# Identity products in TensorE's first idle stretches, and a later place for five denominator groups, in an attention and feed-forward kernel

## The chip, the cores and the metric

The kernel runs on one NeuronCore of a Trainium2 chip. Its engines work side by side: TensorE (PE; its weight loads are listed as PEld), VectorE (DVE), ScalarE (ACT), GpSimd (POOL), and SyncE (SP), whose queue issues nearly all DMAs here. The metric is the device time of one execution in microseconds (us); the figure given is the median of the runs.

## The reference

Attention with normalised queries and keys over 8 batches, 12 heads, 448 positions and a head size of 64, followed by a feed-forward layer with a squared ReLU; everything is fp32.

```python
def rmsnorm(x, g):
    return x / np.sqrt(np.mean(x * x, axis=-1, keepdims=True) + 1e-06) * g
q_n, k_n = rmsnorm(q, g_q), rmsnorm(k, g_k)          # q, k, v: (8, 12, 448, 64)
scores = (1 / np.sqrt(64)) * q_n @ k_n.transpose(0, 1, 3, 2)
attn = np.exp(scores - scores.max(-1, keepdims=True))
attn = attn / (attn.sum(-1, keepdims=True) + 1e-09)
x = (attn @ v).transpose(0, 2, 1, 3).reshape(8 * 448, 768)
h = np.maximum(x @ w_in, 0.0)                        # w_in: (768, 2048)
return h * h @ w_out                                 # w_out: (2048, 768)
```

## The kernel before

**Pairs and units.** Two neighbouring heads of one batch make a pair, so there are 48 pairs, `i` = 0 to 47, six to a batch. The feed-forward layer works on two batches at a time; such a unit has 12 pairs. Its products use Strassen's scheme: seven products P1 to P7 stand for eight, in `first_products` (L705, x by w_in, seven times three matmuls for each of eight tiles of a unit) and `second_products` (L757 and L786, the hidden values by w_out). An fp32 matmul is two instructions in the trace.

**Order of the work.** All instructions are issued in an order written out by hand (`manual_schedule`), each engine in its own order. First the attention of pairs 0 to 11 runs alone (`visit_alone`, two visits a pair). Then `ffn` is a generator that yields after every product, and `run(until)` takes products from it until a cost is spent; between two calls of `run` stands the attention of a pair of the next unit, in two visits for pairs up to 24 (`visit_among`) and in one for later ones (`visit_whole`). So the attention of pairs 12 to 24 lies among the feed-forward products of the first unit, in which `first` is true. During this unit the kernel also converts the weights: the words of w_in and w_out are loaded by SP (L868, L873), split by ScalarE (L887 to L889), joined by VectorE (L900, L920, L924), combined by VectorE and GpSimd (L946) and stored (L948).

**The start.** Before the program proper, the first rows of q and k are loaded (L157, L166), the identity is made in `ident` by GpSimd, and the gains' product goes into PSUM (L95), from where ScalarE takes it as `g` (L100). `normalize_first` squares a row block (ScalarE, L179), adds it up (VectorE, L192, L195), takes the power -1/2 (GpSimd, L202) and scales q (VectorE, L217). Then each engine reads a flag (L101) and branches (L102) into `program`, which is there twice: with `shift` False, which runs here, and with `shift` True. The program sets up memory and starts more loads, and then comes the stretch that the change touches: `turn(0, 1)` and `turn(0, 0)` transpose k and q of pair 0 on TensorE (L362, L365) into bank 6 and bank 7; kT is copied by ScalarE (L372), and qT is scaled by g on VectorE (L370). `score` (L397) multiplies them, and `weigh` (L405) is ScalarE's exponential. For later pairs, square and normalise run on ScalarE, VectorE and GpSimd (L179, L181, L192, L202, L217), before the pair is turned.

**The denominators.** A pair's weights are added up by GpSimd (`additions`, L424) into two sums. `denominators(i)` (L507) multiplies each sum by a matrix of ones on TensorE, into bank 3 for these pairs, and `take_sums` (L549) transposes that bank on VectorE into `inverse`, in a single buffer that it shares with the squares of a later pair. Two tasks queued by the visit, `invert` (L566, L567) and `finish` (L582), run later and end with the pair's values being multiplied. `attend` (L477) multiplies the weights by v. For `visit_among(i, n)` the order on TensorE is: the denominators of pair i - 1 if n is 1 and they are still missing, two slots of `attend(i - 1)`, then the scores of pair i. A pair with odd i has only slot 2 to score in its second visit, into banks 0 and 1; one with even i has slots 2 and 3, into banks 0 to 3. The products of the feed-forward layer use banks 5, 6 and 7.

The main loop calls `denominators(i - 1)` early, between the two `run` calls that precede the second visit, and then the visit finds `inverse` filled:

```python
run(COST * (2 * x - (2 if whole(i - 1) else 1)) / (2 * unit))
...
if n and first and x > 1 and not shift:
    denominators(i - 1)
run(COST * x / unit)
```

## Time and profile before

| what | value |
|---|---|
| median of 4 runs | 1432.3 us (1431.05 to 1433.89) |
| the profiled execution | 1433.92 us; span of its trace 1432.5 us |
| PE busy | 1408.0 us, 98% of the span |
| DVE, ACT, POOL busy | 659.8, 592.7, 677.0 us |
| chain that ended last | PE 92%, DVE 3% |
| PE busy from 0 to 24 us | 14.78 us |
| PE busy from 140 to 520 us (the first unit's products with attention among them) | 376.39 us |
| L507, denominators | 48 instructions, 151.8 to 475.7 us |

The span runs from the first to the last instruction of the trace; the execution's own time is 1.4 us longer. A row of a timeline has the start, the duration, the engine, the line of the kernel, what it writes and reads, and, in brackets, how long the engine stood idle before it and which work ended that. Instructions of one kind that follow each other are merged into a row, whose duration runs from the start of the first to the end of the last, so that it can overlap the next row a little; the distance from start to start is then the cost of a group.

### The profile page before, as it was taken

Reading aid. Unit: us, or ns where it says so; the run is one execution under the profiler, and the core shown is the slowest. Engines: PE = TensorE matmul, PEld = TensorE weight load, DVE = VectorE, ACT = ScalarE, POOL = GpSimd, SP = SyncE. Lnnn points to the kernel's source line nnn. Section 1 sums busy time; section 2 is a strip of 40 time slices with the busy share of each in tenths; the row PEclk is TensorE's granted clock in tenths of the full one; section 3 lists DMA queues with packets and bytes.
Section 4 is the critical chain, followed back from the end, with each engine's and each line's share of the span. In section 5 each row is a group of like instructions: output and inputs, shape, how many; then the busy total and the mean of one; then the engine's idle time right before and its main releaser. Section 6 shows DMA issues by size and latency. Waiting matters only on the chain.

```text
span 1432.5 us, 15428 instructions
## 1 busy us (share of the span) xinstructions
PE 1408.0 (98%) x4932; PEld 681.6 (48%) x4932; DVE 659.8 (46%) x1233; ACT 592.7 (41%) x1114; POOL 677.0 (47%) x676
## 2 busy tenths in 40 slices
PE   7999999999999999999999999999999999999998
PEld 3333444444444445445454544445454455555554
DVE  5997365877778513324252452324233241132413
ACT  6874566547555244442415234351432303212130
POOL 5666654746556656446445565464462422021111
PEclk9999999999999999999999999999999999999999
DMA  5765346665676663443435464343622232313122
GB/s 144 191 195 150 66 103 185 174 199 142 196 204 200 189 178 95 149 115 118 125 65 175 113 186 125 97 131 77 181 70 89 94 154 78 115 51 127 38 88 80
DMA packets 309279, 188.12 MB, mean 131 GB/s; under 512 B 265796, under 2 KB 293316, under 8 KB 300996
## 3 DMA queue, kind: packets, MB, share of 16 engines
q1 hardware_dynamic: 308896, 186.97, 44.6%
q8 instruction: 41, 0.67, 0.2%
q14 instruction: 50, 0.41, 0.1%
q10 hardware_dynamic: 292, 0.07, 0.0%
HBM read 144.57 MB, written 42.40 MB: 131 GB/s over the span
## 4 chain that ended last, share of the span: by engine, by line
PE 92%; DVE 3%; SPq 1%; issue 1%; ACT 1%; POOL 1%; DMA 1%; DVEq 0%; POOLq 0%; ACTq 0%
PE bank L705 36%; PE bank L786 29%; PE bank L477 10%; PE bank L397 9%; PE bank L757 5%; PE bank L490 1%; PE bank L507 1%; PE bank L516 1%; DVE acc L827 1%; SPq L157 1%; PE bank L362 1%; DMA words<-in_moe_w_out_dram 0%; ACT wT L405 0%; SPq L166 0%; DVE out_sb L946 0%
## 5 line engine op out<-in xcount | busy, mean ns | idle before, releaser
L705 PE MATMUL bank<-xT,in_sb 128*128 128x448 f32 x1344 | 515.4, 542 | 0.0
L705 PEld LDWEIGHTS bank<-xT,in_sb 128*128 128x128 f32 x1344 | 252.4, 190 | 260.4 <-issue 250.9
L827 DVE TENSOR_TENSOR acc<-acc,bank 128x384 f32<-128x384 f32 x324 | 173.7, 549 | 233.0 <-PE bank L786 184.9
L786 PE MATMUL bank<-out_sb,hid 128*128 128x384 f32 x768 | 266.6, 487 | 0.5 <-DVE acc L827 0.5
L725 DVE TENSOR_TENSOR hid<-bank,part 128x448 f32<-128x448 f32 x128 | 76.9, 621 | 330.0 <-PE bank L705 329.7
L405 ACT ACTIVATE wT<-bank,rr 128x448 f32<-128x448 f32 x288 | 161.2, 633 | 124.2 <-PE bank L397 73.2
L786 PE MATMUL bank<-out_sb,sums 128*128 128x384 f32 x576 | 203.9, 490 | 2.7 <-DVE acc L827 2.6
L786 PEld LDWEIGHTS bank<-out_sb,hid 128*128 128x128 f32 x768 | 145.4, 190 | 104.4 <-DVE acc L827 2.4
L202 POOL TENSOR_TENSOR rr<-ms,minus_half 128x8 f32<-128x8 f32 (+1 forms) x96 | 146.3, 1524 | 91.5 <-DVE ms L195 78.8
L741 POOL TENSOR_TENSOR sums<-hid 128x384 f32<-128x384 f32 x32 | 32.3, 1008 | 302.1 <-ACT hid L727 302.1
L397 PE MATMUL bank<-qT,kT 64*128 64x448 f32 (+1 forms) x768 | 164.7, 575 | 1.5 <-DVE qT L370 1.1
L726 ACT ACTIVATE hid<-hid 128x448 f32<-128x448 f32 x128 | 73.3, 573 | 196.8 <-DVE hid L725 196.8
L786 PEld LDWEIGHTS bank<-out_sb,sums 128*128 128x128 f32 x576 | 107.7, 190 | 87.1 <-issue 8.1
L712 ACT COPY part<-bank 128x448 f32<-128x448 f32 x128 | 67.8, 530 | 175.6 <-PE bank L705 175.6
L424 POOL TENSOR_TENSOR sum<-sum,wT 128x448 f32<-128x448 f32 (+1 forms) x96 | 110.4, 1171 | 10.8 <-ACT wT L405 8.1
L397 PEld LDWEIGHTS bank<-qT,kT 64*128 64x128 f32 (+1 forms) x768 | 55.6, 174 | 104.8 <-issue 68.0
L477 PE MATMUL bank<-wT,vt 128*64 128x448 f32 x480 | 102.2, 546 | 0.0
L757 PE MATMUL bank<-out_sb,hid 128*128 128x384 f32 x256 | 85.6, 488 | 0.0
L528 POOL COPY few<-few 32x14 f32<-32x14 f32 x48 | 9.1, 189 | 153.3 <-DVE few L526 151.3
L424 POOL TENSOR_TENSOR sum<-wT 128x448 f32<-128x448 f32 x48 | 57.1, 1208 | 50.4 <-ACT wT L405 50.4
L192 DVE TENSOR_REDUCE ms<-squares 128x8 f32<-128x512 f32 (+1 forms) x68 | 41.8, 615 | 76.4 <-ACT squares L179 76.4
L727 ACT ACTIVATE hid<-hid 128x448 f32<-128x448 f32 x128 | 73.8, 577 | 4.0
(96 smaller groups left out, 1281.5 us busy)
## 6 DMA issues: line engine op xcount, KB each, us to landing
out_sb<-out_forms SPq DMA_DIRECT2D x24, 1536.0 KB, 9.7
in_sb<-in_forms SPq DMA_DIRECT2D x24, 1344.0 KB, 5.8
words<-in_moe_w_in_dram SPq DMA_DIRECT2D x32, 384.0 KB, 3.8
words<-in_moe_w_out_dram SPq DMA_DIRECT2D x32, 384.0 KB, 3.7
out_forms<-out_sb SPq DMA_DIRECT2D x8, 1536.0 KB, 7.0
in_forms<-in_sb SPq DMA_DIRECT2D x8, 1344.0 KB, 6.0
qk<-in_q_dram SPq DMA_DIRECT2D x96, 96.0 KB, 3.3
qk<-in_k_dram SPq DMA_DIRECT2D x96, 96.0 KB, 2.5
```

The lines of the kernel that those rows point to most:

```text
L202: self.nc.gpsimd.tensor_tensor(out=self.rr[i][:, x, 0 : self.count(i)], in0=ms, in1=self.minus_half.to_broadcast(list(ms.shape)), op=ALU.pow,)
L397: nc.tensor.matmul(sc[some], lhsT=turned[p, 1][r, keys], rhs=turned[p, 0][r, :], start=True, stop=True,)
L405: nc.scalar.activation(new_weights((i, m), e), sc, AF.Exp, scale=rows.rr[i][:, 1, 2 * m + e : 2 * m + e + 1],)
L424: nc.gpsimd.tensor_tensor(out=sums[i, e][some], in0=left[some], in1=weights[key_of(i, m), e][some], op=ALU.add)
L477: nc.tensor.matmul(values_bank(i)[ds(e * D, D), :], lhsT=lasts[i % 2][mine, e, :] if m == NJ else values[i][:, m, e, :], rhs=weights[key_o ...
L705: nc.tensor.matmul(ps, lhsT=w_sb[:, IN.index(left), c, :], rhs=forms[u, c][right], start=first and c == 0, stop=c == NK - 1, skip_group_ch ...
L725: nc.vector.tensor_tensor(out=dst, in0=left, in1=right, op=op)
L726: nc.scalar.activation(dst, dst, AF.Relu)
L727: nc.scalar.activation(dst, dst, AF.Square)
L757: nc.tensor.matmul(ps, lhsT=flat[a][:, t, ds(NT * P, P)], rhs=w_sb[t][:, 2 * a + half, :], start=(a, t) == parts[0], stop=(a, t) == parts[-1],
L786: nc.tensor.matmul(ps, lhsT=lefts[left][:, t, ts(tt, P)], rhs=w_sb[t][:, OUT.index(right), :], start=first and t == 0, stop=t == 1, skip_g ...
L827: nc.vector.tensor_tensor(out=acc, in0=acc, in1=ps, op=ALU.add)
```

## The change

Three places are edited. Before the gains' product, ten products of the identity by itself are issued into a PSUM tile of their own that nothing reads. In the program, two such products stand before `turn(0, 1)`, five between it and `turn(0, 0)`, and five after, all into bank 5, whose contents nothing reads either. And in the main loop the early call of `denominators(i - 1)` is made for even i only. For odd i (15, 17, 19, 21 and 23; 13 already was so) the group is issued by `visit_among` at the head of the second visit.

```diff
@@ -91,6 +91,10 @@
         gains = psum.tile([P, 1], F32, name="gains")
+
+        nothing = psum.tile([P, P], F32, name="nothing")
+        for _ in range(10):
+            nc.tensor.matmul(nothing, lhsT=ident, rhs=ident, start=True, stop=True)
         for e in range(2):
             nc.tensor.matmul(
                 gains[ds(e * D, D), :], lhsT=g_rows[:, 0], rhs=ones[0:1, 0:1], start=True, stop=True
@@ -1178,8 +1182,15 @@
         if shift:
             rows.scale(0, 1, nc.gpsimd)
+        def idle(number):
+            for _ in range(number):
+                nc.tensor.matmul(banks[5][:, 0:P], lhsT=ident, rhs=ident, start=True, stop=True)
+
+        idle(2)
         turn(0, 1)
+        idle(5)
         turn(0, 0)
+        idle(5)
         for x in range(2):
             rows.normalize_first(1, x, new_acc()[:, 0 : 4 * P])
@@ -1199,7 +1210,7 @@
-                    if n and first and x > 1 and not shift:
+                    if n and first and x > 1 and i % 2 == 0 and not shift:
                         denominators(i - 1)
                 run(COST * x / unit)
```

## The prediction

> **What bounds the kernel now.** I read the page's busy shares first, then the chain that ended last, then the timeline of the first 40 us and TensorE's own timeline from 136 to 300 us, since the two edits lie there.

> ```profile
> PE 1408.0 (98%) x4932; PEld 681.6 (48%) x4932; DVE 659.8 (46%) x1233; ACT 592.7 (41%) x1114; POOL 677.0 (47%) x676
> PE 92%; DVE 3%; SPq 1%; issue 1%; ACT 1%; POOL 1%; DMA 1%; DVEq 0%; POOLq 0%; ACTq 0%
> ```

> TensorE is busy for 98% of the span and holds 92% of the chain: a matmul group removed, or a wait in front of one, is worth its time wherever TensorE is the engine behind. The start is another matter:

> ```profile
> 3.07 0.37 PE L95 MATMUL gains<-ones,g_rows 1*64 1x1 f32 x4 [3.07 <-DVE g_rows L86]
> 7.05 0.87 PE L362 MATMUL bank<-wide,qk 128*128 128x128 f32 x3 [3.60 <-ACT g L100]
> 8.90 0.90 PE L362 MATMUL bank<-wide,qk 128*128 128x128 f32 x3 [0.77 <-DVE qk L217]
> 11.14 3.36 PE L397 MATMUL bank<-qT,kT 64*128 64x448 f32 x8 [1.13 <-DVE qT L370]
> 13.07 1.16 ACT L405 ACTIVATE part<-bank,rr 128x448 f32<-128x448 f32 x2 [3.21 <-PE bank L397]
> 21.03 0.55 PE L362 MATMUL bank<-wide,qk 128*128 128x128 f32 x3 [0.65 <-POOL qk L217]
> 27.95 1.77 PE L397 MATMUL bank<-qT,kT 64*128 64x448 f32 x8
> ```

> Columns are start, duration, engine, line. Four idle stretches (3.1, 3.6, 0.8, 1.1 us) stand before 11.14. Eight score instructions take 3.36 us at 11.14 and 1.77 us at 27.95: half speed, though the granted-clock column reads 1.00 there. Transposes become fast between 15.1 and 15.8 us. From 22 us the chain runs almost wholly along TensorE.

> The denominators (L507), first mid-stream, then the group at the head of a visit, then the one that waits:

> ```profile
> 144.85 7.03 PE L705 MATMUL bank<-xT,in_sb 128*128 128x448 f32 x18
> 151.81 0.97 PE L507 MATMUL bank<-sum,ones 128*64 128x448 f32 x4
> 152.61 0.92 PE L477 MATMUL bank<-wT,vt 128*64 128x448 f32 x4
> ...
> 170.00 4.78 PE L705 MATMUL bank<-xT,in_sb 128*128 128x448 f32 x12
> 174.71 0.97 PE L507 MATMUL bank<-sum,ones 128*64 128x448 f32 x4
> 175.61 4.78 PE L705 MATMUL bank<-xT,in_sb 128*128 128x448 f32 x12
> ...
> 264.97 0.97 PE L507 MATMUL bank<-sum,ones 128*64 128x448 f32 x4 [0.54 <-ACT wT L405]
> ```

> [...]half-speed rows until about 15.7 us; later the granted clock in stretches of 1 us drops to 0.50 from about 107.84 (0.92 in 107 to 108) to 114.66 (0.67 in 114 to 115), 6.82 us[...]. [...]the drop came after 3.9 us (104.92 to 108.83) that held nothing but 1.1 us of transposes. [...]warm transposes with such loads follow each other here at 0.11 us.

> **Part 1: 22 unread products.** An fp32 product is two instructions and two weight loads (L705: 4 x 8 x 7 x 3 products, 1344 rows). No row shows one of 128x128. Lower bound: loads hidden, 128/448 of L705's spacing of 0.1875 us, so 0.11 us a product at full clock. Upper: each instruction paced by its load like the transposes, 0.22. I take 0.22, 0.44 at half clock.

> - Ten products: from the identity's end (POOL, 1.3 to 1.6 us) to about 5.9. They lie in the idle 3.07 and 3.60 us. L95 moves behind them, from 3.07 to about 5.9; its reader, ScalarE's L100, starts at 6.69. Cost nothing.
> - Two products: before `turn(0, 1)` at 7.05. If they don't share its wait they are hidden (0.9 us at most); if they do, they cost 0.44 to 0.9.
> - Five between the turns: `turn(0, 1)` ends at 8.14 and `turn(0, 0)` waits to 8.90. At full clock `turn(0, 1)` takes some 0.45 instead of 1.09 and the five 1.1, so they end by 8.6. At half clock they end at 10.3, 1.4 late.
> - Five before the scores: `turn(0, 0)` ends near 9.4 at full clock, the five end at 10.5. The scores need qT (L370), and VectorE's flag read and branch end at 10.16, so L370 moves only from 10.31 to about 10.2 and the scores to 11.0. Hidden.

> [...]Then the eight scores last 1.5 us plus 0.3; the first weighing starts at 12.1 instead of 13.07 and the last ends near 14.4 instead of 15.67. `turn(1, 0)` stays at 14.43, since it waits for VectorE's scale (13.68 to 14.24), which waits for GpSimd (L202 to 13.64); TensorE idles from 12.5 to then, less than the 3.9 us before the fall at 107.84. Both turns of pair 1 then end at 15.3 instead of 16.1; kT's copy moves from 16.15 to 15.5, the square of pair 2 (L179) from 16.58 to 15.95, its sum, L202 (18.22 to 17.6, GpSimd being held by L181 to 17.31) and the scale L217; TensorE's transposes of pair 2 move from 21.03 to 20.4. ScalarE, busy 6.97 of 7 us from 17 to 24, also starts 0.5 to 0.6 earlier. **Gain 0.6 us**, not the 1.5 us by which the scores shrink: what is late next is GpSimd and VectorE. Bounds: 0.9 (L181 becomes the limit) and none; a loss is rival 3.

> SP's DMA issues don't move in order; those that wait for TensorE shift along.

> **Part 2: five moves.** `denominators(i - 1)` runs early for i = 14 to 24. Odd i from 15 to 23 move: L507 at 205.44, 264.97, 327.39, 387.11 and 446.03 go to the visits at 211.70, 270.58, 333.00, 393.37 and 451.64. Nothing is removed; four TensorE instructions and VectorE's L549 (0.64 us) move, with no DMA.

> Mid-stream, 170.00 to 180.31 is 10.31 us for 24 L705 plus L507; 24 L705 unbroken take 9.22 (616.25 to 625.47): L507 costs 1.09 there (0.75 of streaming, the rest the changes of weights). In L786 the same sum is 11.62 against 10.52: 1.10. At the head L507 takes 0.80 and the following L477 group 1.60 instead of 1.65: 0.75. So 0.345 a move, 1.4 us for four of them.

> The fifth (i = 17) also sheds the 0.54 us wait, 0.9 in all. But VectorE runs unbroken from 270.76 to 286, and TensorE waits for it at 281.58 (0.39) and 284.39 (1.25). VectorE can start only about 0.3 earlier, ScalarE being full from 262.6 to 270.5: I take 0.3. Bounds 0 and 0.9.

> New waits: in a visit with odd i only slot 2 is scored, into banks 0 and 1, not bank 3, which holds the denominators. L549 now stands behind L725 and ahead of `invert`, L566 at 274.97 and later, and the L920/L924 conversions; these give back the 0.64 that they gain from its going. The sums' buffers are asked for again by L424 at 278.44, 7 us after. GpSimd has the sums ready: POOL's additions ended before 258. **Gain 1.7 us**, bounds 0.5 and 2.3.

> **Sum.** 0.6 + 1.7 = 2.3 us. The profiled execution took 1433.9 (span 1432.5 and 1.4 around it), so 1431.6 for it. It is 1.6 above the median of 1432.3, and the cold stretch at 108 cost it about 2.9 (twelve L477 in 4.75 instead of 2.41, twelve L397 in 2.42 instead of 1.87), which may be what spreads the runs over 2.8. From the median: **1430.0 us**, 0.16% less.

> **Rivals.**
> 1. The early clock is hidden: pair 2 waits for GpSimd anyway, as the chain of waits (L217 before 21.03) suggests. Only Part 2 counts: 1430.6. Against: L179's start follows TensorE. 0.22.
> 2. More than the sum: pair 2 gains 0.9, i = 17 its 0.9, and the stretch at 108[...] at 1.3 of its 2.9: 0.9 + 2.3 + 1.3 = 4.5, 1427.8. Against: nothing shortens the 3.9 us gap. 0.27.
> 3. Slower: the clock isn't released by 8.1 us, and the products stand in the way. The two share the wait at 7.05 (0.9), so `turn(0, 0)` starts after the five at 11.2 and ends at 12.3; five more (2.2) put the scores at 14.5, 3.4 after 11.14. Less Part 2's 1.7 that is 1434.0; with Part 2 giving only 0.5, 1435.2.[...] 0.08.

> My sum itself has 0.43.

> **Numbers.** 0.2% is 2.9 us, about what a measurement of this kernel can tell from no change. The sum and rival 1 lie within it; rival 2 is mostly beyond, and a tenth of the sum's own spread as well: faster 0.29, same 0.67, slower 0.04, half of rival 3. Range 1427.6 to 1432.8: rival 2 down to its value, and up to Part 2's low bound with no gain at the start (1431.8) and 1 us for the runs' spread.

> **What would show it.** Right: L362 of the first turns at 0.55 us for three, eight scores at 11 us in about 1.8, pair 2's transposes near 20.4; L507 directly before L477 in five visits, no wait at 265, unbroken groups of 24 L705 in 9.2 us. Wrong: scores at 3.3 us or starting after 12; a wait before L397 in the five visits; the waits near 281 and 284 grown by more than 0.6; TensorE's group starts after 480 us less than 1 or over 4 us earlier.

## The result and the profile after

| | before | after |
|---|---|---|
| median, first comparison | 1432.52 us (1431.0 to 1436.01, 60 runs) | 1430.44 us (1428.53 to 1431.57, 40 runs) |
| ratio | | 0.9985, 95% interval 0.9981 to 0.9990 |
| median, second comparison, on another chip | 1433.18 us (1430.82 to 1435.82, 61 runs) | 1430.37 us (1428.19 to 1431.66, 21 runs) |
| ratio | | 0.9978, 95% interval 0.9972 to 0.9985 |
| span of the first profile | 1432.5 us | 1429.2 us (own time 1430.6) |

The change makes the kernel faster by 2.1 us in the first comparison and by 2.8 us in the second (the differences of the medians). The two intervals overlap from 0.9981 to 0.9985, which is 2.7 to 2.1 us. 2.3 us had been forecast.

Four lines before `normalize_first` are new, so after has L366 where before has L362, L369 for L365, L401 for L397, L409 for L405, L481 for L477, L511 for L507, L709 for L705, L790 for L786, L831 for L827 and L950 for L946. The same holds for all kernels below with the ten products. The ten are L97; the two, five and five are L1187.

In the page of after TensorE has 4976 matmul instructions, 44 more than before (two for each of the 22 products), and 1.5 us more busy time (1409.5 us, 99% of the span), and the span is 3.3 us shorter: the added work lies in former idle time. The timeline of after at the start (start, duration, engine, line; in brackets the idle time before and what ended it):

```profile
1.35 4.06 PE L97 MATMUL nothing<-wide 128*128 128x128 f32 x20 [1.35 <-POOL wide masks.py:199]
...
7.32 0.49 PE L366 MATMUL bank<-wide,qk 128*128 128x128 f32 x3
...
7.76 1.28 PE L1187 MATMUL bank<-wide 128*128 128x128 f32 x10
...
10.96 1.77 PE L401 MATMUL bank<-qT,kT 64*128 64x448 f32 x8 [0.36 <-DVE qT L374]
12.04 1.16 ACT L409 ACTIVATE part<-bank,rr 128x448 f32<-128x448 f32 x2 [2.35 <-PE bank L401]
14.10 0.55 PE L366 MATMUL bank<-wide,qk 128*128 128x128 f32 x3 [1.37 <-DVE qk L221]
...
20.11 0.55 PE L366 MATMUL bank<-wide,qk 128*128 128x128 f32 x3 [0.65 <-POOL qk L221]
```

The first transposes already take 0.49 us for three instead of 0.87, and the eight scores 1.77 instead of 3.36. The first weighing begins 1.03 us earlier (13.07 to 12.04). But the transposes of pair 1 begin at 14.10 behind 1.37 us of idle time, because they wait for VectorE's scale of the rows; at pair 2 what is left is 0.92 us (21.03 to 20.11). Of this, 0.18 us is not the clock's: ScalarE's first square, which waits for the load of q, starts at 4.65 us here and at 4.83 in before.

TensorE in the first unit, around the group that waited at 264.97 before. Behind that group, before had two more waits:

```profile
281.58 1.56 PE L786 MATMUL bank<-out_sb,sums 128*128 128x384 f32 x4 [0.39 <-DVE acc L827]
284.39 1.56 PE L786 MATMUL bank<-out_sb,sums 128*128 128x384 f32 x4 [1.25 <-DVE acc L827]
```

The same place in after:

```profile
258.64 9.29 PE L709 MATMUL bank<-xT,in_sb 128*128 128x448 f32 x24
267.86 0.97 PE L511 MATMUL bank<-sum,ones 128*64 128x448 f32 x4
268.66 0.92 PE L481 MATMUL bank<-wT,vt 128*64 128x448 f32 x4
...
281.96 1.56 PE L790 MATMUL bank<-out_sb,sums 128*128 128x384 f32 x4 [1.26 <-DVE acc L831]
```

The 24 products run unbroken, 9.22 us from start to start, the denominators follow with no wait, and attention after 0.80 us. Of the two waits for `acc` one is left, at 281.96. The list of TensorE's waits between 140 and 520 us has these entries for before, and a single one for after:

```profile
PE bank L786 <- DVE acc L827: 2.6, 3, 1.3
PE bank L507 <- ACT wT L405: 0.5, 1, 0.5
```

```profile
PE bank L790 <- DVE acc L831: 2.2, 2, 1.3
```

Columns: us in total, times, the longest. 0.9 us of waiting is gone, in two places.

### The profile page after: what moved, and what is told of

Read it like the earlier page. It is cut to its first block, busy times and chain, and to the rows that moved or that the text cites. A ratio compares the mean times of both kernels' runs of the same rounds, so it can differ in the third digit from the quotient of the medians.

```text
span 1429.2 us, 15512 instructions
## 1 busy us (share of the span) xinstructions
PE 1409.5 (99%) x4976; PEld 687.3 (48%) x4976; DVE 661.1 (46%) x1233; ACT 591.5 (41%) x1114; POOL 677.5 (47%) x676
## 4 chain that ended last, share of the span: by engine, by line
PE 91%; DVE 3%; SPq 1%; DMA 1%; POOL 1%; issue 1%; ACT 1%; DVEq 0%; POOLq 0%; ACTq 0%
PE bank L709 36%; PE bank L790 28%; PE bank L481 10%; PE bank L401 9%; PE bank L761 5%; PE bank L494 1%; DVE acc L831 1%; SPq L161 1%; PE bank L520 1%; PE bank L511 1%; PE bank L366 1%; DMA words<-in_moe_w_out_dram 0%; DVE in_sb L928 0%; DVE in_sb L904 0%; DMA qk<-in_k_dram 0%
## 5 line engine op out<-in xcount | busy, mean ns | idle before, releaser
L709 PE MATMUL bank<-xT,in_sb 128*128 128x448 f32 x1344 | 514.6, 542 | 0.0
L709 PEld LDWEIGHTS bank<-xT,in_sb 128*128 128x128 f32 x1344 | 252.7, 190 | 259.4 <-issue 252.6
L831 DVE TENSOR_TENSOR acc<-acc,bank 128x384 f32<-128x384 f32 x324 | 173.6, 549 | 231.6 <-PE bank L790 182.3
L790 PE MATMUL bank<-out_sb,hid 128*128 128x384 f32 x768 | 266.5, 487 | 0.5 <-DVE acc L831 0.5
L409 ACT ACTIVATE wT<-bank,rr 128x448 f32<-128x448 f32 x288 | 160.9, 632 | 125.1 <-PE bank L401 73.9
L790 PE MATMUL bank<-out_sb,sums 128*128 128x384 f32 x576 | 203.8, 489 | 2.3 <-DVE acc L831 2.2
L790 PEld LDWEIGHTS bank<-out_sb,hid 128*128 128x128 f32 x768 | 145.4, 190 | 104.5 <-DVE acc L831 2.1
L401 PE MATMUL bank<-qT,kT 64*128 64x448 f32 (+1 forms) x768 | 163.1, 570 | 0.7 <-DVE qT L374 0.4
L790 PEld LDWEIGHTS bank<-out_sb,sums 128*128 128x128 f32 x576 | 107.9, 190 | 85.9 <-issue 8.1
L401 PEld LDWEIGHTS bank<-qT,kT 64*128 64x128 f32 (+1 forms) x768 | 55.2, 172 | 103.4 <-issue 65.6
L481 PE MATMUL bank<-wT,vt 128*64 128x448 f32 x480 | 101.9, 545 | 0.0
```

Source lines behind the costliest of these rows:

```text
L401: nc.tensor.matmul(sc[some], lhsT=turned[p, 1][r, keys], rhs=turned[p, 0][r, :], start=True, stop=True,)
L409: nc.scalar.activation(new_weights((i, m), e), sc, AF.Exp, scale=rows.rr[i][:, 1, 2 * m + e : 2 * m + e + 1],)
L481: nc.tensor.matmul(values_bank(i)[ds(e * D, D), :], lhsT=lasts[i % 2][mine, e, :] if m == NJ else values[i][:, m, e, :], rhs=weights[key_o ...
L709: nc.tensor.matmul(ps, lhsT=w_sb[:, IN.index(left), c, :], rhs=forms[u, c][right], start=first and c == 0, stop=c == NK - 1, skip_group_ch ...
L790: nc.tensor.matmul(ps, lhsT=lefts[left][:, t, ts(tt, P)], rhs=w_sb[t][:, OUT.index(right), :], start=first and t == 0, stop=t == 1, skip_g ...
L831: nc.vector.tensor_tensor(out=acc, in0=acc, in1=ps, op=ALU.add)
```

## The experiments

The theory was the sum: the start's clock is worth 0.6 us, and each moved group saves TensorE 0.345 us. Its rivals were that the start's lead is hidden by GpSimd, that more than the sum is gained because the half-clock stretch at 108 us goes, and that products at half clock stand in the way.

Comparisons over several rounds ran in three sets of four, each set on one chip with its own runs of before (medians 1432.95, 1433.48 and 1433.18 us). Nothing of the computation is left out anywhere; the products of the identity are extra work that nothing reads.

### Each part alone

Part 1 alone is the change with the old condition; Part 2 alone is before with one edit:

```diff
-                    if n and first and x > 1 and not shift:
+                    if n and first and x > 1 and i % 2 == 0 and not shift:
```

> The 22 identity products alone, all denominators left early. Theory (the two parts add up, and the start gives 0.6 to 0.9 us): 0.4 to 0.9 us below before, pair 2's transposes near 20.1 us instead of 21.03, the denominators of pair 16 still waiting near 264. Rival (the early clock is hidden): within 0.2 us of before, and whatever lead stands at 21 us is given back at the wait for the lasts near 106 us.

> The five moves alone, no products. Theory of the prediction: 1.7 us below before. Theory from the trace after: from 137 to 502 us TensorE's group starts gain 2.8 us, so up to 2.8. Rival (they come out of the start's shift): no more than 1 us. The first 21 us must look like before: eight scores in 3.4 us.

Part 1 alone: 1432.67 us, ratio 0.9999 (0.9991 to 1.0008). Part 2 alone: 1431.6 us, 0.9987 (0.9980 to 0.9994). The moves carry the gain that can be measured; the start's part lies inside an interval that allows from 1.3 us of gain to 1.1 us of loss. The start of each is as expected: pair 2's transposes at 20.16 us in Part 1 alone, and the eight scores still 3.36 us long in Part 2 alone. But in Part 1 alone the denominators of pair 16, left early, no longer wait: their group runs at 262.44 without a pause, which was not expected.

A third kernel moves the group of i = 17 alone (`i != 17` in place of `i % 2 == 0`):

> Only the denominators before pair 17's second visit are moved. Prediction: 0.3 us below before, since VectorE is full from 270 us. Rival, from the trace after: 1.4 us, 0.35 of weight changes, 0.54 of the wait near 265, 0.39 of the wait near 281.

It gave 1432.81 us, 0.9997 (0.9989 to 1.0005). Its trace answers better than its time: the stretch from the start of the first products to the second products behind the moved group is 0.95 us shorter than in before (273.19 - 136.78 = 136.41 against 270.06 - 134.60 = 135.46), and over the whole first unit 0.55 is left (404.83 against 404.28, the distance that the next section defines). The waits for `acc` grew from 2.6 to 3.0 us, so VectorE takes back 0.4. A single pair of profiles is a weak basis, as the next section shows.

### The first unit, measured from its own beginning

Spans mix the moves with what happens before 136 us. I therefore compare one distance in all profiles, from the first L705 (L709) to the fifth group of second products, where the attention of the last moved pair is past:

| no group moved | us | five moved | us | all eleven moved | us |
|---|---|---|---|---|---|
| before | 404.83 | after, first profile | 401.99 | without products | 402.33 |
| Part 1 alone | 404.23 | after, second profile | 402.02 | with products | 403.98 |
| before with nine products at 106 us | 404.41 | after with the nine | 402.86 | with products and the nine | 404.27 |
| Part 1 with the nine | 405.26 | Part 2 alone | 402.93 | | |
| Part 1 without the ten | 405.79 | | | | |
| the ten alone | 405.62 | | | | |

From there to the end all 14 take the same time to 0.4 us (890.8 to 891.1). Pairs that differ by the five moves alone give 1.90 us (before and Part 2 alone), 2.24 (Part 1 alone and after) and 2.40 (Part 1 with the nine, after with the nine). The spread of 1.6 us within the first column, where nothing moved, is mostly TensorE's listed waits, which add up to 2.58 to 3.81 us there. With the waits taken off, the first column reads 401.64 to 402.06 us (401.82 on the mean), i = 17 alone 401.28, and the four profiles with five moves 399.78 to 400.09 (399.90). So five moves take 1.92 us of work from TensorE, 0.38 a move. The waits are 3.21 us on the mean of the first column and 2.55 with five moves; together that is 2.57 us.

The waits differ between executions. The one of 0.54 us at 264.97, which the move of i = 17 was to remove, stands in before alone; of the other five profiles in which nothing moved, three wait 0.24 to 0.98 us at the group of i = 23 and two at none.

### Which of the products does it

Without the ten, only the two, five and five:

> The kernel before with two, five and five products in the program, but without the ten ahead of the gains. Rival 3 of the prediction (the products run at half clock and stand in the way): the second turn of pair 0 starts near 10.5 instead of 8.9 us, the scores near 12.5 to 14 and pair 2's transposes after 21 us; no gain or up to 2 us slower. Otherwise, if the clock comes in time all the same: transposes of pair 2 near 20.1 and 0.3 to 0.9 us faster.

Its timeline:

```profile
8.91 2.18 PE L1184 MATMUL bank<-wide 128*128 128x128 f32 x10
10.93 0.49 PE L363 MATMUL bank<-wide,qk 128*128 128x128 f32 x3
...
12.58 1.77 PE L398 MATMUL bank<-qT,kT 64*128 64x448 f32 x8
```

(With one new line ahead of them, its lines are one higher than in before.) Five products occupy TensorE at half clock from 8.91 to 10.93 us, 0.20 us an instruction, and stand ahead of `turn(0, 0)`. The scores come at 12.58 instead of 11.14, pair 2 at 21.14, and the time is 1433.29 us, 0.9999 (0.9991 to 1.0007). This is the mechanism of the third rival, and it costs far less than was worked out for it: the clock came up at 10.80, and what was lost before that is hidden up to pair 2.

The ten alone (in the diff, L97's loop stays and the three calls of `idle` go):

> The ten products before the gains alone; none between the turns, no denominators moved. If the ten are what brings the clock up and the other twelve only fill: first scores at 11.0 us, pair 2's transposes at 20.2 to 20.5, and a time of 0.5 to 0.9 below before at most, within 0.2% of it. If TensorE loses the clock again without the twelve: the scores after 11.2, pair 2 at 20.6 to 21.1, and no gain.

```profile
11.52 3.36 PE L401 MATMUL bank<-qT,kT 64*128 64x448 f32 x8 [1.12 <-DVE qT L374]
...
21.69 0.55 PE L366 MATMUL bank<-wide,qk 128*128 128x128 f32 x3 [0.20 <-POOL qk L221]
```

In this profile the ten released nothing: the scores run at half clock and pair 2 is 0.66 us late, 0.39 of it because q landed later (first square at 5.22 against 4.83). The median is 1434.01 us (1430.54 to 1434.88) and the ratio 0.9999 (0.9991 to 1.0007). Neither half of the products gives a gain that the times show. That the ten alone never release the clock isn't shown by one profile, for the next point.

### The clock comes up at another time in each execution

All eleven groups at the head of the visit, and the change's products with them, made one kernel; without the products, another:

```diff
-                    if n and first and x > 1 and i % 2 == 0 and not shift:
+                    if n and first and x < 0 and not shift:
```

The kernel with the products has the same start as after, instruction for instruction. Its timeline:

```profile
1.35 4.64 PE L97 MATMUL nothing<-wide 128*128 128x128 f32 x20 [1.35 <-POOL wide masks.py:199]
...
8.69 2.31 PE L1187 MATMUL bank<-wide 128*128 128x128 f32 x10
...
12.48 1.77 PE L401 MATMUL bank<-qT,kT 64*128 64x448 f32 x8
...
21.04 0.55 PE L366 MATMUL bank<-wide,qk 128*128 128x128 f32 x3 [0.65 <-POOL qk L221]
```

Here the ten ran at half clock throughout (4.64 us against 4.06 in after), five products took 2.31 us against 1.28, and pair 2 begins at 21.04, as in before. Six of the seven profiles with all 22 products had the clock before the first transposes, and this one at 10.8. It moves without the products too. All eleven at the head without products:

```profile
14.44 0.59 PE L362 MATMUL bank<-wide,qk 128*128 128x128 f32 x3
```

The transposes at 14.44 are fast already, where before's at 14.43 took 0.90 us, and pair 2 comes at 20.48, which is 0.55 us of the start's gain for nothing. Each of the 14 traces keeps the moments at which the granted clock changed (ahead of the first, the column of the views reads 1.00): without products it first rose between 14.56 and 16.03 us, with all 22 at 4.17 to 5.97 in six profiles and at 10.84 in this one.

Within one trace all changes of the clock lie a whole number of stretches of 3.413 us apart. In before it rose at 15.68, fell at 107.84, 27 stretches later, and rose again at 114.67, two later. So the changes of each trace lie on a grid of such stretches, whose position against the kernel's start differs: the first edge lay between 0.56 and 2.56 us in the 14 profiles. At the start of these profiles the clock rose behind the first stretch in which TensorE was busy for 2.81 us or more. Stretches with up to 2.73 us released nothing, nor did one with 2.86, of which 0.38 are the gains' products of a single column. In after the edges are at 1.25 and 4.66, and the ten, from 1.35 on, fill the stretch between them. In the kernel with all eleven groups and the products they are at 0.60, 4.01, 7.43 and 10.84: the ten fill only 2.66 us of the first stretch and end at 5.99, in the middle of the second. The ten alone met nearly the same edges (0.59, 4.01, 7.42), and there the clock rose only at 17.66.

So in six profiles it is the ten that released the clock: it had risen by 5.97 us, before the first of the other twelve. In the seventh, where they fill 2.66 us of the first stretch, it rose at 10.84, and without the ten at 10.80, both times while the twelve ran.

Counted from the first square of q, so that its load drops out, pair 2's transposes begin after 15.46 or 15.47 us in the six profiles with the early clock, after 16.18 in the seventh with all products, and after 15.63 to 16.37 (16.08 on the mean) in the five with before's start. The early clock is worth 0.6 us at pair 2, and 0.5 on the mean of the seven.

### The even visits

> All eleven denominator groups of the first unit at the head of the second visit, no products. Theory (with even i the visit scores slot 3 into bank 3, which VectorE must have read first): in the six visits with even i TensorE waits before its second group of scores, 1 to 3 us each, and the kernel is slower than with the five moves alone, at or above before. Rival (VectorE reads bank 3 in time): another 6 x 0.35 = 2.1 us below the five moves alone, so 3.5 below before.

> The change with all eleven groups of denominators at the head of the second visit, not five of them. If a move is worth what it frees also for even i: about 0.6 us below the change as it is, and 2.6 below before. If bank 3 makes the even visits wait each time, five waits of 2.1 us at the scores (L401) against five times 0.35 gained: 8 us above the change. If it does so in one visit in six as in the profile of all heads alone: between level and 0.6 below.

Without products: 1431.08 us, 0.9987 (0.9978 to 0.9996). With them: 1431.96 us, 0.9990 (0.9984 to 0.9997), beside after itself, which ran in the same set:

> The change as it is, beside the next three. If its gain is the sum of its parts: about 2.0 us below before, between 1.2 and 2.8, with the first products of the first unit at 134 to 136.2 us and the stretch from there to the fifth group of second products at 402.0 to 403.0 us. If the 2.84 us that this stretch gave in its first profile were all due to the five moves, it reads 402.0 again; if about 0.9 of it came from how VectorE and GpSimd happened to meet, it reads anything from 402.0 to 403.0.

After's first unit took 402.02 us this time, so the 401.99 of its first profile was no accident. Moving the even groups too made the change worse, by 1.6 us (1430.37 to 1431.96); the two intervals, 0.9972 to 0.9985 and 0.9984 to 0.9997, overlap by a hair only. None of my prices was right: five waits would have cost 8 us, and one wait or none would have given up to 0.6. One visit waits, and it is the same in all three profiles of this kind. From the timeline of all eleven with products, TensorE and VectorE:

```profile
298.61 0.55 PE L511 MATMUL bank<-sum,ones 128*64 128x448 f32 x2
...
303.91 0.64 DVE L553 STREAM_TRANSPOSE inverse<-bank 128x448 f32<-128x448 f32 x1
304.60 1.77 PE L401 MATMUL bank<-qT,kT 64*64 64x448 f32 x6 [2.10 <-DVE inverse L553]
```

The denominators are in bank 3 at 299.16. VectorE frees the bank only at 304.55, behind the conversions of the weights in its queue (the last, L928, took 1.26 us from 302.72), and the scores of the even pair, which need bank 3, stand for 2.10 us. In the other even visits no wait for `inverse` is listed.

With the products this wait also brought the clock down, in both profiles. Here is the kernel of the rows above over two stretches of its grid (start and end, length, time that TensorE was busy, number of its instructions, granted clock, and two columns on DMA):

```profile
300.97:304.38 3.41, 1.53 (x6) 1.00 1.13 346
304.38:307.80 3.42, 3.20 (x9) 0.50 0.98 342
```

From the scores behind the wait to the end of the twelve products that follow, 6.40 us passed here and 6.54 in the kernel that has the nine products too, instead of 4.88 without products. There the same wait lay across an edge, with 2.48 and 2.26 us of work in the two stretches, and the clock held. So the wait costs 2.1 us, and the fall behind it 1.5 to 1.7 more. Where the clock held, all eleven took 402.33 us in the first unit, 0.60 less than Part 2 alone, so that the six even groups gained more than their wait cost. With the fall they took 403.98 and 404.27, against 402.02 and 402.86 with five moves. How often the clock falls there in other executions is not shown.

### VectorE and GpSimd meet in one place

Part 2 alone and i = 17 alone keep a wait for `acc` near 281 us that after doesn't have. In front of it stands one VectorE instruction, here in before and in after:

```profile
278.44 1.14 POOL L424 TENSOR_TENSOR sum<-wT 128x448 f32<-128x448 f32 x1
278.53 1.47 DVE L946 TENSOR_TENSOR out_sb<-out_sb 128x384 f32<-128x384 f32 x1
```

```profile
277.00 0.55 DVE L950 TENSOR_TENSOR out_sb<-out_sb 128x384 f32<-128x384 f32 x1
277.05 1.36 POOL L950 TENSOR_TENSOR out_sb<-out_sb 128x384 f32<-128x384 f32 x1
```

In before VectorE starts 0.09 us behind a GpSimd addition and ends 0.42 after it; in after it is 0.05 ahead of GpSimd's next and takes its 0.55. In before, ten of VectorE's 32 instructions of L946 took 0.82 to 1.49 us; each of them began inside a TENSOR_TENSOR of GpSimd and ended 0.41 to 0.42 us behind its end. The other 22 took 0.52 to 0.55 us. What holds the ten is not shown. Over all profiles the instruction near 278 us took 0.55 us in the five profiles of programs that have all the products and the move of i = 17, and 1.46 to 1.48 us in the nine others. TensorE waits near 281 us, 0.37 to 0.97 us, in all nine of these and in none of the five. So in these profiles the meeting is avoided where the two parts come together; how 22 products at the start have a part in it is not explained.

### The stretch at 108 us

Nine products of the identity before the attention that waits for the last values of pair 9, in `visit_alone(10, 0)`, were meant to keep the clock up:

```diff
+            if i == 10 and not shift:
+                for _ in range(9):
+                    nc.tensor.matmul(
+                        values_bank(i - 1)[:, 0:P], lhsT=ident, rhs=ident, start=True, stop=True
+                    )
```

> The changed kernel with nine more unread products just before the values of pair 9 in pair 10's first visit, where TensorE waits some 2.5 us for the lasts near 106 us. Theory ([...]the clock is halved for 6.8 us, which costs 2.9): the stretch at half clock near 107 us is gone, the median is 1 to 1.5 us below the changed kernel's, so 3 to 3.6 below before. Rival (the products take the time or the stretch hides behind later waits): no lower than the changed kernel, 2.1 below before.

> The kernel before with the nine products ahead of pair 9's values and nothing else. Theory (the stretch at half clock near 107 us costs some 2.3 us by the start of the first unit's products, in about half of the runs): 1 to 1.4 us below before, no stretch at half clock after 100 us, first unit's products starting near 134.6 us instead of 136.8. Rival (the stretch is covered by later waits): within 0.3 us of before.

> The 22 products at the start and the nine ahead of pair 9's values, no moves. Theory (the start gives 0.8 to 1.0 us, which the first experiment hid because its longer wait at 106 us brings the half clock more often): 0.8 to 1.0 us below the kernel with the nine alone, so 1.8 to 2.4 below before. Rival (the start's lead is taken by the wait for the lasts): no lower than the kernel with the nine alone.

> The change, the nine products ahead of the wait for the last values, and all eleven groups at the head. If the parts add up: 0.6 us below the change with nine products, which was at 0.998 of before, so 3.4 us below before; span 1426.5. If the even visits' waits and the wait at 108 us each take their share again: 2.0 to 2.9 below before.

| nine products added to | us | ratio to before | without the nine |
|---|---|---|---|
| before | 1433.29 | 1.0000 (0.9991 to 1.0010) | 1 |
| Part 1 | 1432.02 | 0.9993 (0.9985 to 1.0001) | 0.9999 |
| after | 1429.63 | 0.9980 (0.9973 to 0.9987) | 0.9985 and 0.9978 |
| all eleven with products | 1430.6 | 0.9981 (0.9973 to 0.9988) | 0.9990 |

No row is clear of its neighbour by its interval; the last one, both kernels in one set, shows 1.4 us. Against before the forecasts were 1 to 1.4 us for the first row, which is missed, and 3 to 3.6 for the third, where the medians give 3.3 and the ratio 2.9. The second row was to lie 0.8 to 1.0 below the first, in its own set, and lies 1.3 below; the last was to lie 2.0 to 2.9 below before if its waits take their share, and the medians give 2.6. Timelines of after with the nine, and of before with the nine:

```profile
105.63 2.27 PE L1077 MATMUL bank<-wide 128*128 128x128 f32 x18
108.49 0.97 PE L481 MATMUL bank<-wT,lasts 128*64 128x448 f32 x4 [0.59 <-DMA lasts<-in_v_dram]
```

```profile
106.40 2.27 PE L1073 MATMUL bank<-wide 128*128 128x128 f32 x18
110.63 0.97 PE L477 MATMUL bank<-wT,lasts 128*64 128x448 f32 x4 [1.96 <-DMA lasts<-in_v_dram]
```

In after the nine fill the wait up to 0.59 us, and the clock stays at 1.00. In before the load of the values, issued at 106.59 us, took about 4.0 us, against 2.4 in the profile without the nine (issued at 106.39, values in use at 108.83). TensorE waited another 1.96 us, and the clock fell at 111.60. Three of the four profiles with the nine keep the clock, and two of the ten without them (i = 17 alone, and all eleven without products).

The stretches of the grid tell these profiles apart too. In the nine profiles with a fall near 108 us, the stretch ahead of it had 0.13 to 1.58 us of work for TensorE; in the five without one, every stretch had 1.79 or more. Before, with a wait of 2.45 us, and i = 17 alone, with one of 2.65 that lies across an edge:

```profile
104.43:107.84 3.41, 1.58 (x12) 1.00 0.70 157
107.84:111.25 3.41, 2.42 (x8) 0.50 0.80 253
```

```profile
103.98:107.39 3.41, 1.86 (x14) 1.00 0.72 159
```

The same holds over the whole of the 14 traces: the clock fell behind no stretch with 1.7 us of work or more, and behind all with 1.6 or less but one (1.56 us, i = 17 alone, near 280 us).

The fall lasts two stretches, 6.8 us, in before, Part 2 alone and the first profile of after, and one, 3.4 us, in the six others. From pair 2's transposes to the first unit's products it is 112.98 to 113.76 us in the five profiles without a fall, 114.69 to 116.21 with one stretch and 115.75 to 116.00 with two: 1.8 and 2.5 us more on the mean, where 2.9 had been estimated for before. These means also contain differences in when the values landed. That the fall widens the runs is only in part supported: in four of the five profiles without it the time is the lowest or second lowest of its kernel (1428.67, the lowest of 19, with the nine in after), but those 19 runs still range over 2.9 us.

## Why the prediction was right

The predicted 1430.0 us stands against 1430.44 and 1430.37, the gain of 2.3 against 2.1 and 2.8. Point by point:

- **Price of a product.** Taken at 0.22 us, 0.44 at half clock. Ten instructions take 1.12 us from start to start at full clock (7.76 to 8.88), 0.11 each and 0.22 a product; at half clock 0.21 each where the five go from 8.69 to 10.82 us, and 0.23 in the twenty of 4.64 us, 0.42 to 0.46 a product. The upper bound held: the products go at the pace of the transposes, 0.11 us apart.
- **The ten and the start.** The scores at 10.96 (11.0 predicted), the first weighing at 12.04 (12.1), `turn(1, 0)` at 14.10 (14.43 kept), pair 2 at 20.11 (20.4). The clock came at 4.66 us; that it would come before the scores was the author's estimate, shown by no trace of before. The term of 0.6 measured 0.6 with the early clock and 0.5 on the mean of the seven. What the working missed is that both ends vary with the grid: it took the rise at 15.7 us from before's one profile as fixed, and it lay between 14.56 and 16.03. That the first profile had well-placed edges was luck, with odds of six in seven here.
- **Transposes and the clock.** The fall at 107.84, which the prediction puts after 3.9 us with 1.1 us of transposes, came within that gap, 2.9 us after the last score. In these traces transposes count as work for the clock. Before's clock rose at 15.68 behind a stretch with 2.16 us of scores and 1.25 of transposes, while 2.73 us of scores in a stretch of the ten alone released nothing. With i = 17 moved alone, the clock held behind a stretch with 1.86 us of work, 1.09 of it transposes; in the second profile of after it fell behind one with 1.31. The fall at 107.84 fits the 1.58 us of work in its stretch, transposes counted.
- **Moves at 0.345.** With the waits taken off, five moves measured 0.38 each, 1.92 us instead of 1.73.
- **i = 17, and Part 2 as a whole.** This is the mis-sized term: 1.7 us forecast for Part 2, with 2.3 as its upper bound. It measured 1.90 to 2.40 in single pairs of profiles and 2.57 on the mean of the columns. The step that failed is the account of the waits. The 0.54 us at 264.97 was taken for a part of the kernel and stands in one of six profiles in which that group stayed early. And VectorE was to begin only 0.3 us earlier because it runs unbroken from 270.76. That holds for the moves alone, where the wait near 281 grows from 0.39 to 0.83. But 0.9 us of the unbroken stretch was the longer L946 beside GpSimd's addition (1.47 us against 0.55), and in all five profiles with both parts this went, and the 0.39 us with it.
- **No new wait for odd i; even i would need bank 3.** The five moved visits show no wait at the scores. The even ones do in one visit out of six, 2.10 us, and the fall of the clock that followed it in two of three profiles was not foreseen.
- **Rival 1**, the early clock hidden: no; 0.5 to 0.6 us gets past GpSimd up to pair 2, though it can't be seen in the times of Part 1 alone. How much of it reaches the end is not shown.
- **Rival 2**, more than the sum: half of it came. Fewer waits around i = 17 are there; the stretch at 108 us is in both profiles of after.
- **Rival 3**, products in the way: it happens, without the ten and in one profile with them. Its price was wrong: it put the scores at 14.5, and they came at 12.48 and 12.58, since the clock rose at 10.84 and 10.80, while the products ran. At pair 2 the two are 0.01 and 0.11 us behind before. So it can take the start's gain away, and not turn the whole into a loss.

**Open:** what else spreads the runs of one kernel over 2.5 to 7.5 us; why the values landed later in before with the nine products; what holds VectorE beside GpSimd in L946, and how the products at the start keep the two apart at 277 us; whether the ten alone, where they release the clock, also keep it up to the scores.

## What to carry to other kernels

An edit that saves two thousandths is read in the stretch that it touches, from a fixed instruction before to one behind, with the listed waits taken off: here the work that the moves save then shows as 1.9 us against a spread of 0.4, where single spans mixed it with up to 3 us of clock and waits. Put a short group where its operands are old and other short groups stand (here 0.75 us at the head of a visit against 1.09 amid equal products), and ask at each place which buffer it occupies until a busy engine frees it; the move that saves 0.38 us cost 2.1 in one even visit, and a fall of the clock behind it. Here the clock rose behind the first stretch of 3.41 us with 2.81 us or more of work (one of 2.86 apart), and the first edge lay anywhere from 0.56 to 2.56 us. By an estimate from these figures, 3.41 + 2.81, or 6.2 us of unbroken products, would fill such a stretch wherever the edges lie; the ten last up to 4.64, brought the early clock in six profiles of seven, and so their gain is a mean over executions, not a fixed amount.
